# A state-space convolution with gated linear attention on one core: another table for the order of all steps, the engines of evictions and the PSUM rings

## The chip, the cores and the metric

The kernel runs on one core of a Trainium2 chip. The metric is the device time of one execution in microseconds; the median of 3 runs of the kernel before is 265.66 us (265.65 to 267.71). Of the engines, PE is TensorE, DVE VectorE, ACT ScalarE, POOL GpSimd; SP is SyncE, which here only issues DMAs.

## The reference

One input u (1 x 2048 x 512) goes through two branches, which a gate per token mixes into an output of the same shape in bfloat16.

```python
x = A_u                                  # 1 x 2048 x 512, bfloat16
g = _sigmoid((x * gate_w).sum(-1, keepdims=True))
# branch a: per channel d a kernel K of 2048 taps from 128 complex modes, applied as a causal convolution (FFT of length 4096)
P = jnp.exp(logdA[:, :, None] * l[None, None, :])
K = jnp.einsum("dn,dnl,dn->dl", Cc, P, dB).real
y = irfft2(rfft2(up) * rfft2(Kp))[:L]  + u * Dskip
# branch b: 32 heads of 16, feature map phi(q) = [softmax(pq), softmax(-pq)], pq = q @ w_phi per head, no softmax over tokens
kv = einsum("bhsf,bhsd->bhfd", phi_k, v);  z = phi_k summed over s
o = (phi_q @ kv) / (phi_q @ z + 1e-6);  b = o.reshape(B, S, D) @ wo
```

The output is the two branches a and b, mixed token by token with g and 1 - g.

## The kernel before

**Branch a** is worked in 16 units of 32 channels. Four units make a block Q of 128 channels. A unit runs through these steps:

- Tables. TensorE makes arguments (args, L1023 for the sines cs, L1045 for the exponentials E) from statC or statE and a selector table selE (L458); ScalarE turns them into cs and E; VectorE multiplies E into its second half (L1053), builds the products A (L1101, two of 128x2048) and R (L1119, L1123, one each). For 8 of the 16 units, named by the string FOURS, TensorE sums four terms itself; for the other 8, VectorE first halves A by an addition (L1112).
- Kernel taps. TensorE multiplies A and R into kps (L183), the result is evicted as KD.
- Forward transform in two stages: psA (L190), evicted as XA; psB (L196), evicted as XK.
- VectorE multiplies XK with the spectrum of the input, XUX, to t (L1233, L1236). XUX is loaded from DRAM through SyncE (L1186, L1188) into a ring of three.
- Inverse transform: psz (L1265), evicted as Zr, written to DRAM (Zd, L1278) and read back transposed as ZT (L1287). TensorE turns ZT into psy (L1343). VectorE multiplies the result by the gate into xT (L1365, L1368, L1371); in part it goes through a copy into Ctab. The last unit is small enough to stay on the chip: its psz (L1299) is evicted as Z and used directly (L1356). The stores are those of L1382.

**Branch b** runs over 4 blocks of 512 tokens. First for all keys and values: pk (L709) and its exponential Ek on ScalarE, vp (L757) evicted as vb, and their products kvp (L774). Then for the queries: pq (L843), the exponentials Eq, their sums through DRAM (apd, L899; ax, L906), the product Eq by ax on VectorE (L913), ops (L932), and the output product bps with wo (L946, to which L948 and L949 add the convolution's share). The bps are evicted in pieces: a plain copy to xT, and a gated piece of 128x384 by ScalarE (L981) or VectorE (L983), which the store of L995 sends out. The fourth block of tokens is done late, beside the last units.

**What sets the order.** The class Plan (from L71) collects each step as a node with its engine, what it depends on, which buffer rings it takes and gives back. Three strings then decide what is issued where. ORDER holds two digits of base 64 for each node and is the order in which all nodes are emitted; each engine, and each DMA queue, gets its own steps in that order and works them in order. SIDES has a digit for each node that may go to one of two engines: an eviction to ScalarE (L149) or VectorE (L151), the selector table selE and a few others to VectorE or GpSimd, a store to SyncE's or ScalarE's queue. RINGS has a digit for each node that may take its PSUM tile from one of two rings. Nothing in the kernel's functions changes with these strings, only place and engine. The line of Plan.copy that chooses is:

```python
def copy(self, o, i):
    if self.cur.at == "ACT":
        self.nc.scalar.copy(out=o, in_=i)
    else:
        self.nc.vector.tensor_copy(out=o, in_=i)
```

A DMA queue is worked in order too: an issue that waits for its data holds up the issues behind it.

Of the kernel before, what the change touches and what calls it, by code (L numbers as in the profile page):

```python
# [70 lines left out]
class Plan:  # L71

    DIGITS = "0123456789abcdefghijklmnopqrstuvwxyzABCDEFGHIJKLMNOPQRSTUVWXYZ-_"
    ORDER = ("040B0H0K0d0y0C0D0L0s0I070J0M0P0g000S110j0N08010z0T0m0Q0e2R0a0p0q0r0_0W2T100U0O0V14120Y2U2x0A2S050k130Z2y2V2X2Z0R190v0t0u"
             "0b0c0w2_0l0E0X2W1516172L1a061b2Y022-30311y33340n030f0-"
             "0h1e1f0i1w2J18321c0F0o2B2K2M1n1z1H1g1A1o2D2C1d1p1I091x1E1J351Q1R2F1B0x1C2E0G2H1q36372G2I2P382N2Q391F3b2O3c4C1S3a4J4L4K4M"
             "3d3e4Q4R3f4U1Y3g4N1r4O1h4V3h1L4Y4-"
             "4P3i4Z4_3j4W4S53542z57504T3k4X1Z515b5d58521s1D593l5c3n5i5e55565j3m5a1G3o5q5f5g5s5r5t3p3r3q1T5m5n5u3s5v5h5o5k5w5x5B1P4D4E"
             "3w2v5l5p4F5y5F5C3y1U5H3x5G5I5J5z5A1V5D5E3t3z5U3D5K5V5M5N3A3R3E2w3F5W5L1O5_3G5O5Q5X5Y5Z3B3C1W605R5S1N3K3M1K3S1M5-"
             "5P3L634G642A615T653N673T6869626a666m6n6o3U6p3V3W3X3Y6b6c6q6d6r6s1t3Z3H3-1X3_3O1i1j41401_4221431-"  # L80
             "1k1l204445466e272923222b282d4748243P491m2a4a2c2e4b4g2f4c2g4d252h2o4e4h4i4n1u4j3u3v2j4p2i2l2k2m2q2p6i262s4q4o1v4k2n4u2r2t"
             "6f4v4w6j4r3I2u4x4y4z6g4l8l3J4A8p8m6t6u6k6v8q3Q4f4s6x6h8k8o6l8n8r8s6y6z6w6A6C4m4t4B8C6G8t6I6K8w8x8y8u6B6H6J4H8D8v6L6M6N7d"
             "8z8A8E4I8B7e7f8I7g8F6F9e8Q8G8H9b6O6P8R7h7j7i6Q6R8J9f7M7N8S6S6T6U6Vaeaf7O8W8X8K7k9g8L8T8U8Z8-"
             "938M8N7l6D8_7m8V7n6W6X6Y8O8P8Y7P94an7o7pao7q6_70717r90917Qa47S9295ag7R6Z7s6-"
             "72aha8a9966Ea7akaca5ai73aa75979998ajap7677a69aalatamab74ad7TaBaC7t797u7v7U78au7y7z7V7w7x9caq9naras7AavaH7W9d9h9o9paw7X9v"
             "aY9waK7Y7ZaDaL9q9raZ7a9x9y9zaIc57B7-aM9kc69D9EaQaEbX9L7Cb_aF7D9M7_9Ac07EaRaG9iaxaz80ay9B818285bYaA7Ga-"
             "7IaJ86879j9Fc19s7Jb-"
             "9l9m9Na_7bc7aNaOaPc3cbb2b37HbZc283aS9C7FaT849G9H9I9t89aUaWaV8baX7cccc8c99O9u9P9Q9R888cb87Kb9b0c4caceb19J8abacfcgbg8dck9K"
             "8ecl8f8gbbbh8hbcbibob4cP9Sbpbqcd9T8ichci7L8jcBcCcjcsdYcYctcucycDczdZd-cQcR9Ucmd_cHcvcw9W9Xcnbj9VbwbkblbxcocIbre0eLcp9Ze1"
             "e2b5b6eMbse3eUeVcxb7bye4cqbtbu9Ybdbe9-"  # L90
             "9_cAcrcSbme5cZdOdScEbfcFcGcTcUe6a0a1bve7dTdRdWeNa2e8cJcKe9bzbAedeecLeRcNcOa3eSeaebeOcMc_ePbBd0ecd1d7cVd8d9cWeCdfcXeWdPdU"
             "d2daefege-e_eQd3dbdQdgeTdVd4dndodXdhdcg1g2dieDeEdjeXbKfAbCbnbDbEbFeYfBeZf0f1bGc-dpbLddg7dqbHd5f2drbMf3f4f5bNfGbIbJbOezdk"
             "eAfDdsfEeBeIf6f7feffdldtbPdebQdBfCfHehdueifFejdmf8fgeJd6ekdvfIfJdyf9fafhfbg4fifKg5g6dwfjdzfkfcdxdCdEfLdAdFfMg3g8dGg9dHfN"
             "fleFelfdfmfpdDdLgagbgcgddIeGemeKfqeHfOfPfQfRgeenepfneofreqeresgfggghgifSfTfUfofsbRgjbSgkdJftetglfVfYfZgmgngobUbVgqfufWdM"
             "dNbWgpf-fvfxfygreufwevewexbTeydKfzfXf_g0gvgwgsgtgugx")
    SIDES = ("011111010010101011001110110010011001010100001011100000000000011000011001111101000100000100000000000000000000000010000000"
             "00100001000000000000000101010000000000000100001101001")
    RINGS = ("001010111111010010100000000000000000000000100000000000000000001101100000000101101011100100100001101010111100111001010100"
             "01111")
    WARM = ("000000000000000000000000000000000000000000000000000000000000000000000000000000000000000000000000000000000000000000000000"  # L100
            "000000000000000000000")
    FOURS = ("0111100101011000")
# [50 lines left out]
    def run(self):  # L153
        code = {d: i for i, d in enumerate(self.DIGITS)}
        order = [64 * code[a] + code[b] for a, b in zip(self.ORDER[0::2], self.ORDER[1::2])] or list(range(len(self.nodes)))
        assert sorted(order) == list(range(len(self.nodes)))
        sides, rings, warm = iter(self.SIDES), iter(self.RINGS), iter(self.WARM)
        for n in self.nodes:
# [1469 lines left out]
```

## Time and profile before

| what | value |
|---|---|
| median of 3 runs | 265.66 us (265.65 to 267.71) |
| span of the profiled execution | 263.7 us |
| that execution's own time | not given apart from the span; the median stands 1.96 us above it |
| DMA | 35.93 MB, 134 GB/s over the span |
| TensorE steps of the chain that ended last | 32% of the span |
| VectorE steps of that chain | 26% |
| ScalarE steps of that chain | 13% |
| DMA steps of that chain | 12% |

The profile page has the busy time of each engine, the span in slices, the DMA queues, the chain of waits that ended last, and the costliest groups of instructions. The prediction also uses tables of the span cut into stretches, and the timeline of one engine. In the chain a row is a stretch of work, in the order of time; a bracket at the end of a timeline row is the idle time before it and what ended it. The engine that the profile calls SPq or ACTq is the DMA queue of SyncE or ScalarE.

### The profile page before, as it was taken

To read this page: it belongs to the slowest core of one execution; us is meant where nothing else is said; L and a number is where in the kernel's file an instruction comes from. 1 tells how busy PE (TensorE), PEld (TensorE's weight loads), DVE (VectorE), ACT (ScalarE), POOL (GpSimd) and SP (SyncE) were. 2 spreads that over 40 slices of the span, in tenths; PEclk is the share of its full clock that TensorE was granted. 3 is DMA by queue.
4 is the path that set the end of the run, shared out by engine and by line. 5 is a ranking of instruction groups with operands and counts; after the bars stand their busy time and mean duration, and the time that the engine had idled before them with its cause. 6 is when DMAs were issued, how large, how long until landed. Compare 5 with 4: busy or idle time off the path is not lost.

```text
span 263.7 us, 10050 instructions
## 1 busy us (share of the span) xinstructions
PE 198.5 (75%) x4491; PEld 133.8 (51%) x4512; DVE 233.9 (89%) x315; ACT 221.3 (84%) x305; POOL 8.3 (3%) x21
## 2 busy tenths in 40 slices
PE   0755999999845688988565867889996678979770
PEld 0654656646634423446354245665674456764550
DVE  6799989888799989999999999999999999986630
ACT  6989999998899989998999899999998996744200
POOL 4700000000000000000000000000000000000000
PEclk9999999999995659997999579999999999998975
DMA  6899000454500885203343366239753599989576
GB/s 196 144 204 233 6 4 2 121 146 138 151 10 2 239 239 165 83 13 87 88 162 82 122 209 210 73 116 199 150 193 120 189 239 242 179 206 141 133 112 102
DMA packets 67547, 35.93 MB, mean 136 GB/s; under 512 B 46000, under 2 KB 62000, under 8 KB 67504
## 3 DMA queue, kind: packets, MB, share of 16 engines
q1 hardware_dynamic: 65648, 34.76, 55.0%
q10 hardware_dynamic: 1856, 0.52, 1.1%
q8 instruction: 35, 0.57, 1.0%
q14 instruction: 8, 0.07, 0.1%
HBM read 22.17 MB, written 13.11 MB: 134 GB/s over the span
## 4 chain that ended last, share of the span: by engine, by line
PE 32%; DVE 26%; ACT 13%; DMA 12%; issue 7%; SPq 7%; DVEq 0%; ACTq 0%
PE pk L709 5%; DMA ax<-apd 5%; PE vp L757 5%; DVE A L1101 3%; SPq L1494 3%; DMA ZT<-Zd 3%; DMA apd<-apm 3%; ACT cs L68 3%; DVE R L1123 2%; DVE R L1119 2%; PE psz L1265 2%; PE psA L591 2%; PE bps L946 2%; PE psB L616 2%; PE kvp L774 2%
## 5 line engine op out<-in xcount | busy, mean ns | idle before, releaser
L1101 DVE TENSOR_TENSOR A<-Ctab,Dtab 128x2048 bf16<-128x2048 bf16 x32 | 37.9, 1220 | 0.0
L68 ACT ACTIVATE cs<-args 128x1024 bf16<-128x1024 f32 x32 | 30.8, 1042 | 1.5 <-PE args L1023 1.5
L1265 PE MATMUL psz<-t,TI 128*128 128x512 bf16 x51 | 16.5, 414 | 6.2 <-DVE t L1233 4.6
L1123 DVE TENSOR_TENSOR R<-E,cs 128x2048 bf16<-128x2048 bf16 x16 | 19.5, 1219 | 0.1
L1119 DVE TENSOR_TENSOR R<-E,cs 128x2048 bf16<-128x2048 bf16 x16 | 19.5, 1219 | 0.0
L68 ACT ACTIVATE Ek<-pk 128x512 bf16<-128x512 f32 x32 | 16.7, 600 | 1.9 <-PE pk L709 1.6
L183 PE MATMUL kps<-R,A 128*32 128x64 bf16 x1536 | 17.2, 203 | 1.5 <-DVE A L1112 0.4
L183 PEld LDWEIGHTS <-A 128*32 128x32 bf16 x1536 | 15.3, 117 | 5.6 <-issue 2.0
L149 ACT CAST Zr<-psz 128x1024 bf16<-128x1024 f32 x15 | 15.5, 1032 | 3.2 <-PE psz L1265 1.5
L149 ACT CAST XA<-psA 128x1024 bf16<-128x1024 f32 (+1 forms) x15 | 14.7, 1017 | 3.4 <-PE psA L190 3.4
L757 PE MATMUL vp<-WW,xT 128*128 128x512 bf16 x59 | 16.9, 419 | 0.5 <-issue 0.3
L616 PE MATMUL psB<-XAu,TB 64*128 64x128 bf16 x256 | 11.8, 250 | 6.6 <-ACT xst L149 3.5
L1233 DVE TENSOR_TENSOR t<-XUX,XK 128x2048 bf16<-128x2048 bf16 x14 | 16.7, 1219 | 0.0
L68 ACT ACTIVATE E<-args 128x1024 bf16<-128x1024 f32 x16 | 16.4, 1036 | 0.3 <-PE args L1045 0.2
L68 ACT ACTIVATE Eq<-pq 128x512 bf16<-128x512 f32 (+1 forms) x28 | 16.5, 694 | 0.1
L149 ACT CAST XK<-psB 128x1024 bf16<-128x1024 f32 (+1 forms) x14 | 13.7, 993 | 2.8 <-PE psB L196 1.5
L843 PE MATMUL pq<-xT,Wqp 128*128 128x512 bf16 x64 | 15.4, 379 | 0.8 <-ACT xT L149 0.6
L709 PE MATMUL pk<-WW,xT 128*128 128x512 bf16 x58 | 15.0, 380 | 0.4 <-issue 0.2
L190 PE MATMUL psA<-W,KD 128*64 128x128 bf16 x256 | 10.7, 233 | 5.5 <-ACT KD L149 2.7
L616 PEld LDWEIGHTS <-TB 64*128 64x128 bf16 x256 | 9.7, 111 | 9.9 <-issue 9.8
L196 PE MATMUL psB<-XA,TB 128*128 128x128 bf16 (+2 forms) x192 | 10.6, 206 | 3.6 <-DVE XA L151 1.6
L190 PEld LDWEIGHTS <-KD 128*64 128x64 bf16 x256 | 8.5, 117 | 9.1 <-issue 5.2
(210 smaller groups left out, 502.0 us busy)
## 6 DMA issues: line engine op xcount, KB each, us to landing
XUX<-XUd SPq DMA_DIRECT2D x32, 256.0 KB
XUd<-xst SPq DMA_DIRECT2D x8, 512.0 KB
ax<-apd SPq DMA_DIRECT2D x16, 256.0 KB
Zd<-Zr SPq DMA_DIRECT2D x15, 256.0 KB
ZT<-Zd SPq DMA_DIRECT2D x6, 512.0 KB
UD<-in_A_u_dram SPq DMA_DIRECT2D x16, 128.0 KB
XUd<-xst SPq DMA_DIRECT2D x8, 256.0 KB
wqk<-in_B_wqkv_dram SPq DMA_DIRECT2D x1, 1024.0 KB
```

What stands on the lines that cost most here:

```text
L68: return self.nc.scalar.activation(**kw)
L149: self.nc.scalar.copy(out=o, in_=i)
L183: nc.tensor.matmul(kps[32 * dj:32 * dj + 32, g4, e, :], lhsT=A[:, d // 4, 32 * ka:32 * ka + 32, d % 4], rhs=R[:, kr, d, :], start=(i == 0) ...
L190: nc.tensor.matmul(ps[64 * ri:64 * ri + 64], lhsT=lhsT, rhs=fc.W1[:, ri].rearrange("p r d -> p (r d)"), start=True, stop=True, tile_positi ...
L616: nc.tensor.matmul(box.ps[:, c2, sl, :], lhsT=fc.TB[rows, b0:b0 + 2].rearrange("p a b -> p (a b)"), rhs=X.t[rows, k, r0 + sl].rearrange("p ...
L709: nc.tensor.matmul(box.ps[:], lhsT=xT[:, st, kt, :], rhs=g.WW[:, kt, :], start=(kt == 0), stop=(kt == 3))
L757: nc.tensor.matmul(box.ps[:], lhsT=xT[:, st, kt, :], rhs=g.WW[:, 4 + kt, :], start=(kt == 0), stop=(kt == 3))
L1101: nc.vector.tensor_tensor(out=c.A[:, :, 64 * k:64 * k + 64, :].rearrange("p q (x b) l -> p x b q l", b=8), in0=cf.unsqueeze(2).to_broadcas ...
L1119: nc.vector.tensor_tensor(out=c.R[:, :, :, 32:64], in0=t.E[:, 1].unsqueeze(1).to_broadcast([128, 2, 32, 32]), in1=t.cs[:], op=ALU.mult)
L1123: nc.vector.tensor_tensor(out=c.R[:, :, :, 0:32], in0=t.E[:, 0].unsqueeze(1).to_broadcast([128, 2, 32, 32]), in1=t.cs[:, ::-1, :, ::-1], o ...
L1233: nc.vector.tensor_tensor(out=box.t, in0=Ls[r0 // ns].X[:], in1=box.XK[:].unsqueeze(1).to_broadcast([128, 2, 1024]), op=ALU.mult)
L1265: nc.tensor.matmul(box.ps[:, hb, :], lhsT=fc.TI[:, k].rearrange("p t h a -> p (t h a)"), rhs=box.t[:, k, 512 * hb:512 * hb + 512], start=( ...
```

## The change

The three strings ORDER, SIDES and RINGS are replaced; FOURS, WARM and ZPS and every function are the same. The source after is four lines shorter, so that a line number after it is four less than before (L1101 is then L1097). The strings are long, and a line of each shows their kind:

```diff
 class Plan:
...
-    SIDES = ("011111010010101011001110110010011001010100001011100000000000011000011001111101000100000100000000000000000000000010000000"
-             "00100001000000000000000101010000000000000100001101001")
+    SIDES = ("111110110010111010001100101000101000111000001011110000000000111110110001001110000010001000000000000000000000000000000000"
+             "00000000000000000100000000000000000000000001011110101")
-    RINGS = ("001010111111010010100000000000000000000000100000000000000000001101100000000101101011100100100001101010111100111001010100"
-             "01111")
+    RINGS = ("100100101110111011000000000000000000000000100000000000000000111101000000001010101111100111010001001100101011001111100110"
+             "11000")
     FOURS = ("0111100101011000")
```

By these strings, counted over the whole program: VectorE loses two wide evictions XK and one wide XA (128x1024), the selector table selE (to GpSimd, behind Wphi), one bps copy of 256 and the two gated pieces of L983; it gets a copy Ctab of 512, a KD of 256, one XA and one XK of 512, one vb and one copy UDp. ScalarE has the other side of it. Eight of ten vb evictions of VectorE now stand early, of the nine before five. The stores of ScalarE's queue are two instead of four.

The end of VectorE's program, from the last unit's exponential (E, L1053) on, before:

```order
L1053 TENSOR_TENSOR E<-E,Gtab 128x1024
L1123 TENSOR_TENSOR R<-E,cs 128x64x32
L1365 TENSOR_TENSOR xT<-psy,gT 128x4x128
L151 CAST XK<-psB 128x1024
L1368 TENSOR_TENSOR xT<-psy,gT 128x8x128
L1236 TENSOR_TENSOR t<-XUX,XK 128x2x512 x2
L151 CAST XA<-psA 128x32x16
L983 TENSOR_SCALAR xT<-bps,gT 128x384
L151 CAST xT<-bps 128x2x128
L983 TENSOR_SCALAR xT<-bps,gT 128x384
L151 CAST XK<-psB 128x512
L1236 TENSOR_TENSOR t<-XUX,XK 128x2x512 x2
```

and after:

```order
L1049 TENSOR_TENSOR E<-E,Gtab 128x1024
L1097 TENSOR_TENSOR A<-Ctab_75,Dtab 128x64x8x4
L1119 TENSOR_TENSOR R<-E,cs 128x64x32
L1108 TENSOR_TENSOR A<-A 128x8x256
L1361 TENSOR_TENSOR xT<-psy,gT 128x4x128
L147 CAST Ctab_74<-psy 128x4x128
L147 CAST KD<-kps 128x256
L1232 TENSOR_TENSOR t<-XUX,XK 128x2x512 x2
L1364 TENSOR_TENSOR xT<-psy,gT 128x8x128
L147 CAST XA<-psA 128x32x16 x2
L147 CAST XK<-psB 128x512
L1232 TENSOR_TENSOR t<-XUX,XK 128x2x512
```

What moved: both halves of XA and of XK are now VectorE's, the gated pieces are gone from it, the first KD half has come, and the wide XK is gone.

ScalarE around its last change of function table (the row ACT_TABLE_LOAD, after which it makes the last exponentials E), before:

```order
L149 CAST XK<-psB 128x1024
L65 ACT_TABLE_LOAD
L68 ACTIVATE E<-args 128x1024
L149 CAST Zr<-psz 128x2x8x64
L68 ACTIVATE E<-args 128x1024
L149 CAST KD<-kps 128x1024
L149 CAST Zr<-psz 128x2x8x64
L149 CAST XA<-psA 128x32x32 x2
```

and after:

```order
L145 CAST XK<-psB 128x1024 x2
L65 ACT_TABLE_LOAD
L68 ACTIVATE E<-args 128x1024
L145 CAST KD<-kps 128x1024
L145 CAST Zr<-psz 128x2x8x64 x2
L145 CAST oT_4888<-ops 128x1024
L145 CAST XA<-psA 128x32x32 x2
L68 ACTIVATE E<-args 128x1024
```

Between the first and the second E there now stand a KD, two Zr, an oT and two XA, where there was one Zr.

SyncE's queue at the end, before:

```order
L1278 DMA Zd_64_123<-Zr 128x1024
L1382 DMA out_dram<-xT 32x12x256 x2
L995 DMA out_dram<-xT 32x4x384 x2
L1287 DMA ZT<-Zd_64_123 64x32x32 x2
L1382 DMA out_dram<-xT 512x1x64 x4
L995 DMA out_dram<-xT 32x4x384 x2
L1382 DMA out_dram<-xT 512x1x64 x2
```

and after:

```order
L1274 DMA Zd_64_123<-Zr 128x1024
L1378 DMA out_dram<-xT 32x12x256 x2
L991 DMA out_dram<-xT 32x4x384 x2
L1283 DMA ZT<-Zd_64_123 64x32x32 x2
L1378 DMA out_dram<-xT 32x12x128 x2
L1378 DMA out_dram<-xT 512x1x64 x4
L991 DMA out_dram<-xT 32x4x384 x2
L1378 DMA out_dram<-xT 512x1x64 x2
```

Two stores of 32x12x128 have come behind the last ZT loads; two more of 32x12x256, formerly on ScalarE's queue, stand above the piece shown, ahead of the last Zd write.

More of the change, by code (lines that the diff above doesn't have):

```diff
@@ L73 @@
     DIGITS = "0123456789abcdefghijklmnopqrstuvwxyzABCDEFGHIJKLMNOPQRSTUVWXYZ-_"
[L74 to L95, printed above, removed]
@@ L96 @@
-    SIDES = ("011111010010101011001110110010011001010100001011100000000000011000011001111101000100000100000000000000000000000010000000"
-             "00100001000000000000000101010000000000000100001101001")
-    RINGS = ("001010111111010010100000000000000000000000100000000000000000001101100000000101101011100100100001101010111100111001010100"
-             "01111")
+    ORDER = ("190H0I0405060B0C0D0d0e0f0y0z0A0s0t0u000K0L1d0J0M0S0U0V0N0_0P0Q2R11122x0O100W0T13142S0X0Y162T2U0708090g0h0i0j0k0l2y010203"
+             "0m0n0o0a0b0c2V2X0Z15171a1H1b2v0R0-2Y2Z2W2L1c1n1o0p0q0r1w2M2-2_181y302J2K1e1f1p1z1A1I1J2w2B1x1E2D35312E1g1Y2C0v0w0x0E0F0G"
+             "2F321N1B2G2H1C2I33361P372P1O2N341F382Q393b1q1r1s2O4C2z3c4J4K4L4M3d4Y4Z4-3a3e4N4O4_3f4Q3h3g1D4U3j4P1R4R4V4W4S5350573k4T3i"
+             "511S544X52555b5c5d5e3l1G581Q3n595i5f5m3m5g3o1T5n5h5j565a3p3r3s5o1U3q3R5k3S5q5r5s5x1L4D5t3w4E3y5u3x3t3u3v5l5p5B5y5F1V5v5H"
+             "3D1M5C3z2A5w5G3F5z5A5D3G4F5E5I5U5V5W3T3A3B3C3E5X5J5M5N5K5L5O4G5Q5Y5R5Z3K3M5S3U5_1Z635P5T3N5-1h1i1j1k1l1m6067691W643V6162"
+             "65683H3I3J666m3W3L6o3O3P3Q3X3Z3-6a6n6p3Y6b6c1K6q3_6d6r6s414043421X441-27201_4546474828492129224a23246e2d2b252a4b4g4c2e2c"
+             "2f2h1t1u1v266f2j2g4i4d4e4f2i4h4j4k4l4m4n2o2l2q2p6i2k2s4o4p4q4r4s4t2r6j4u4w4v4x2m2t2n6g6k6t4y4z4A6x6u2u8n6y6v4B8r6z8k8o8m"
+             "8q6h6l6w6A6B8l6G8w4H8x8p8t4I6F8s8u6I6K8y6H8z6L8v8A8C9e9f9g8Q6M7d8D8I8E6N6J8R8B7f9b9c9d7g8F6O7h7j6P8S7i8G6Q8H8J8W8Z7Ma_b0"
+             "b17k8K7e6R6S8T6C6D6E7O8-7Q6T8_8L7N7R8M8X6U6V6W937l8O8U8N8V7mae7S8P8Yaf7n7o94907p9192agan7Taoa4ap7q7P6X6Y6Z6_70716-7r7s7t"
+             "a8a995a572ak73ah7u7v7w96aaa6ab9774at98aial7y7z7A7599a776aj9a7x77acau78am797aaqar9n9o7C9v7Uadasav9w7V9paw7B9xaKaLaBaC7D7W"
+             "9q9raHaD9y7X7YaIaQaE9z9D9E7E7F7Zc5c6bXb_9L9Mc0aM7b9k9l9maFaxay9h9i9j9F7-7_80aGazaA7GbYc1aJ7HaR9A9B9C818283858687aNaOaP7I"
+             "7cb-aYaZa-7JaSc784c3aT9Ncb88bZc8899s9t9uc29GaU9H9O8aaVc98b8dc49P9I9J9Kcc8fceaW8gcfaX7Kb5b6b78e8ccacdb8ckb97Lcgch8h8ibg8j"
+             "cBclcibabhcCdYdZbocjcmbpcncDcHbicscvd-cIeLbb9Q9R9S9T9U9Vctcubjcyb2b3b4d_e0bq9W9X9YbccScTcU9Ze1e2eMbwbdbebfcwbke3co9-bxe4"
+             "cPcQcRe5cqczblbmbncxe6e7e8cpbycreUdOeVcVcWcXcAcE9_cFcGa0eNa1dRcJe9eaebdSdTeRdWbrcKbscLcNeOePeSecbzcMcOc_bAdPdQedeeefeWd0"
+             "dUeQbtbubvd1a2d7a3egd8bBbCbDeTdVcYcZc-d2e-d9dad3dfdneXbEbFbGdbe_bKeYbLdgdheZdodXfAf0d4d5d6dcdddefBdpbMdidqf1djehdrfCeibN"
+             "fDf2bHbIbJf4g1f3eCeDeEdkdldmdsdtduf5bOf6fGg2fEf7fHfefFg7fIezeAeBfJffdBg4f8fgfKbPg3f9g5g8g6fLfadvdwdxbQfhdCdydzdAfbfcfddE"
+             "fMdFfiejfNdGg9fjfkfldHekeFeGeHgaeleIeJeKgbepfmfnfoemgcfOfpfqfrfPeneofQbRbSbTeqerdDdIdJdKgdgegfgggifsghgjfRfSfTfUbUbVbWgk"
+             "eseteuevfVfWfXfYfZf-glgmgngodLdMdNftfxfyfzgpfufvfwewexeygqgrf_g0gsgtgugvgwgx")
```

## The prediction

> **What bounds the kernel now.** I read the page's table of engines first, then the span cut into stretches, then the chain that ended last, and at the end the queues that issue the stores. Times without a unit are microseconds. The page's busy line (time, share, instructions):
>
> ```profile
> PE 198.5 (75%) x4491; PEld 133.8 (51%) x4512; DVE 233.9 (89%) x315; ACT 221.3 (84%) x305; POOL 8.3 (3%) x21
> ```
>
> No engine is full over the whole span, so the stretches decide. Their columns are the length, the busy time of PE, PEld, DVE, ACT and POOL with counts, the granted clock, the DMA share and GB/s:
>
> ```profile
> 0.00:30.00 30.00, 15.84 (x170) 13.37 (x172) 25.48 (x58) 26.42 (x34) 8.33 (x21) 1.00 0.88 172
> 30.00:70.00 40.00, 39.47 (x733) 24.24 (x738) 34.88 (x50) 36.95 (x71) 0.00 (x0) 1.00 0.31 88
> 70.00:100.00 30.00, 19.53 (x244) 12.06 (x243) 28.70 (x50) 27.58 (x33) 0.00 (x0) 0.72 0.42 116
> 100.00:215.00 115.00, 88.70 (x2306) 57.80 (x2312) 113.03 (x125) 110.19 (x144) 0.00 (x0) 0.94 0.49 139
> 240.00:250.00 10.00, 7.68 (x185) 4.66 (x185) 5.64 (x10) 3.52 (x6) 0.00 (x0) 1.00 0.80 143
> ```
>
> From 30 to 70 TensorE is busy 39.47 of 40: what VectorE or ScalarE save there is hidden. From 100 to 215 VectorE is busy 113.03 of 115 and ScalarE 110.19: VectorE is the bound, ScalarE a close second with 4.81 to spare. After 240 neither is loaded; the tail is a chain of short steps, as the chain that ended last shows (start, length, what):
>
> ```profile
> 210.97 7.98 DMA ZT<-Zd
> ...
> 236.13 0.94 PE psB L196 x32
> 237.07 0.98 PE kps L183 x48
> ...
> 241.23 0.59 PE psA L190 x16
> 241.84 0.59 ACT XA L149
> 242.46 0.70 DVE XA L151
> 243.20 1.02 PE bps L946 x4
> 244.44 0.86 PE bps L946 x4
> 246.02 0.59 ACT xT L981
> 246.63 0.62 DVE xT L983
> 247.25 0.61 DVE XK L151
> 247.88 1.32 DVE t L1236 x2
> 249.25 3.16 PE psz L1299 x120
> 252.43 0.70 DVE Z L151
> 253.16 0.59 ACT Z L149
> 253.79 0.64 PE psy L1356 x64
> ...
> 256.59 0.69 DVE xT L1368
> ```
>
> The last unit's kernel rows (kps, 16th unit) are done at 238.05 and its inverse transform (psz) starts at 249.25: 11.20 for three small matmul groups and their evictions, with the last attention output (bps) woven in. The last VectorE step ends at 257.28, yet the span is 263.7: the rest is stores (start, length from first issue to the end of the last, queue, line).
>
> ```profile
> 253.16 5.56 ACTq L1382 DMA_DIRECT2D out_dram<-xT  x4
> ```
> ```profile
> 251.63 6.97 SPq L1382 DMA_DIRECT2D out_dram<-xT  x4
> 258.64 1.10 SPq L995 DMA_DIRECT2D out_dram<-xT  x2
> 259.84 1.26 SPq L1382 DMA_DIRECT2D out_dram<-xT  x2
> ```
>
> The store of the last tile is issued at 259.84, 2.56 after that tile is ready, because SyncE works off four older issues and two of L995 first.
>
> **The change part by part.** Lengths come from these groups (busy, mean ns) and from single rows of VectorE's own timeline (start, length), of which the last vb eviction and the wide evictions are shown:
>
> ```profile
> L149 ACT CAST XA<-psA 128x1024 bf16<-128x1024 f32 x14 | 14.1, 1048 | 0.4 <-PE psA L190 0.4
> L149 ACT CAST XK<-psB 128x1024 bf16<-128x1024 f32 x13 | 13.1, 1024 | 1.5 <-PE psB L196 1.5
> L151 DVE CAST vb<-vp 128x512 bf16<-128x512 f32 x9 | 6.1, 687 | 1.9 <-PE vp L757 1.9
> ```
> ```profile
> 57.67 1.22 DVE L458 TENSOR_TENSOR selE<-m,b 128x1024 bf16<-128x1024 bf16 x1
> 98.50 0.68 DVE L151 CAST vb<-vp 128x512 bf16<-128x512 f32 x1
> 171.66 1.22 DVE L151 CAST XK<-psB 128x1024 bf16<-128x1024 f32 x1 [0.40 <-PE psB L196]
> 202.21 1.22 DVE L151 CAST XA<-psA 128x1024 bf16<-128x1024 f32 x1
> 234.34 1.22 DVE L1123 TENSOR_TENSOR R<-E,cs 128x2048 bf16<-128x2048 bf16 x1
> ...
> 237.11 1.23 DVE L151 CAST XK<-psB 128x1024 bf16<-128x1024 f32 x1 [0.25 <-PE psB L196]
> ```
>
> 1, the VectorE stretch. Two evictions leave VectorE for ScalarE inside 100 to 215, the XK at 171.66 and the XA at 202.21: 2 x 1.22 = 2.44 less there (the third wide one, at 237.11, belongs to the tail). Two of the late vb evictions (four before, two now, by the order) go as well, 2 x 0.687 = 1.37, but ahead of 100 (the last is at 98.50), where TensorE's clock is 0.72 and much waits on it; I count them at nothing, and the bound is 2.44 + 1.37 = 3.81. ScalarE takes 1.024 + 1.048 = 2.07 more in the stretch, of its 4.81 to spare. The room is there, but its queue is in order and a moved eviction now stands behind others; I give back a fifth: **-2.0** (ends 0 and -3.8; at 0 ScalarE is the bound).
>
> The selE product at 57.67 goes to GpSimd, and more vb evictions come to VectorE in the early part (eight against five). Both lie in 30 to 70 or before; TensorE's 39.47 of 40 covers them: 0. Without that cover they would cost 3 x 0.69 - 1.22 = +0.8. The new order of the first 30 (sine table work, XUX loads) has the same fate: the DMA share is 0.88 there and TensorE's full stretch begins on what these loads bring: 0, ends -1 and +1.
>
> On GpSimd selE stands behind Wphi:
>
> ```profile
> L473 POOL TENSOR_TENSOR Wphi<-wc,mask 128x512 bf16<-128x512 bf16 x1 | 1.1, 1056 | 4.3 <-DMA wc<-in_B_w_phi_dram 4.3
> L269 DVE TENSOR_SCALAR tgv<-tgc,one 128x1024 int32<-128x1024 f32 x2 | 2.6, 1286 | 2.2 <-ACT TB L68 2.2
> L269 DVE TENSOR_SCALAR tgv<-tgc,if,one 128x1024 int32<-128x1024 f32 x2 | 1.6, 808 | 0.0
> ```
>
> Twice as wide as Wphi, I take 2 x 1.06 = 2.1 of GpSimd for it. A VectorE step of nearly the same form takes 1286 ns where GpSimd runs beside it and 808 where it doesn't, so VectorE may lose about 0.5 per such step, one or two steps, in the hidden part: 0, bound +1. The Trainium skill, "SBUF — State Buffer", section "Who interferes with whom", says that the port pair of VectorE and GpSimd is an exclusive lock, so that one fully blocks the other. By that rule VectorE would stand up to 2.1 rather than 0.5; the rows show a loss of about half of the GpSimd step, less than the rule, and the sum stays as it is, since the place is covered.
>
> 2, the tail chain. Before, two bps groups stand ahead of psA and two between psA and psB, and gated evictions of ScalarE (0.59) and VectorE (0.62) stand ahead of XK. Now all four groups follow kps at once, all four gated evictions are on ScalarE, and VectorE takes both halves of XA (0.70 each) and of XK (the same shape, 0.65 taken), each XK half followed by its own product t. From kps's end at 238.05: four bps groups at 1.1 each (the pair from 243.20 ends at 244.44 + 0.86 = 245.30, so 1.05 a group), 4.4; psA 0.59; XA 2 x 0.70; psB 0.94; XK twice, 1.3, and t twice, 1.32. Sum 4.4 + 0.59 + 1.4 + 0.94 + 2.62 = 9.95 with no waits, against 11.20: 1.25 less, of which I keep a wait of 0.25 back, **-1.0**. Ends: 0, if ScalarE's gated evictions leave the PSUM ring late and TensorE's third group waits for a buffer; -2, if the second halves overlap fully. The VectorE product of psy that moves behind Z (1024 wide, 1.22 like the evictions of that width) falls into the time of the second Z half on ScalarE and the psy group behind it (253.16 to 254.43, 1.27): it costs nothing, and up to 1.2 if that cover is gone. VectorE also gets the first KD half and one Ctab copy of 512; with 5.64 busy of 10 after 240 and the bps groups on TensorE behind kps, they are covered, and 0.4 and 0.7 without that.
>
> 3, the stores. ScalarE's queue has two stores of 32x12x256 and two of 512x1x64; the wide ones go to SyncE, ahead of the last ZT loads, and two of 32x12x128 now stand behind these loads. Behind the last ZT loads SyncE then makes 10 issues instead of 8; the two more cost 1.10 / 2 = 0.55 each (the row at 258.64), 1.1 in all, if SyncE still is behind at the end. On the other side the wide transfers move out of the last 11 and no longer run beside the last stores. I take **0**, ends +1.1 and -1.5 (half of the 2.56 of backlog and some). The Trainium skill, "DMA: Bandwidth & Descriptors", section "Issuing engines are not separate DMA queues", says that transfers of all issuing engines run on the same 16 DMA engines and that a second issuing engine only saves issue time. By that the move can't slow the transfers and costs the 1.1 of issue at most. No row here shows the two cases side by side.
>
> 4, new waits. The table lets the two last exponentials (E of units 14 and 15) come later on ScalarE beside VectorE's order. Adding the groups' mean lengths along each order, an estimate of mine puts the slack between E of unit 14 and its VectorE step at about 8 before and about 0 now. If each of the two E, of the kind and length of a cs step (1.04, the row under the second rival), stands in VectorE's way for a quarter of that, it is **+0.5** (bounds 0 and +2.1); queued behind it on VectorE stand the last A and R products, for which kps and the tail wait. Of SyncE's queue, the first half of the ZT load at 210.97 (7.98 to its landing, in the chain) moves ahead of two Zd writes and the second stays behind them: 0, and up to -1.5 if that landing still sets TensorE's start.
>
> Sum on the profiled execution: 263.7 - 2.0 - 1.0 + 0 + 0.5 = 261.2 of span. The median 265.66 lies 1.96 above this span (the page has no other time for the profiled execution), so **263.2**; as the first two terms have longer ends below (-3.8, -2) than above, I lean by half a microsecond: **262.7** us, 1.1% less.
>
> **The rivals.** First, no change by swallowing: ScalarE becomes the bound. For it: 110.19 of 115 busy, +2.07, and its exponentials now last in line. Against: 4.81 idle. Then term 1 is 0, term 2 is halved by the same ScalarE work ahead of the gated evictions: 265.66 - 0.5 + 0.5 = **265.7**.
>
> Second, slower: the transform loop turns on ScalarE's order. From 100 to 215 each unit's KD, XA and XK evictions sit in ScalarE's queue between table work of this kind:
>
> ```profile
> L68 ACT ACTIVATE cs<-args 128x1024 bf16<-128x1024 f32 x32 | 30.8, 1042 | 1.5 <-PE args L1023 1.5
> ```
>
> If the three moved 1024-wide evictions each wait behind one such step and run there, VectorE's next t product waits 1.04 + 1.02 = 2.06 each, 6.2 in all, against 2.44 saved; with the tail gain gone because E of the last unit is late too (+1.0), the time is 265.66 - 2.44 + 6.2 = 269.4, less what VectorE's other ready work fills: **269**. It decides if VectorE's idle time in 100 to 215 goes over 2 + 2.44 + 2.7 = 7. Against it: before, ScalarE carries 27 such wide evictions of XA and XK (14 and 13 by the groups) behind just such steps, and VectorE still is busy 113.03 of 115.
>
> Third, the change doesn't do what its words say: the table that chooses units whose sums go to TensorE is the same in both, A products and their halving steps have equal counts, and so nothing comes from that. This is sure, and is in the sum as 0. What remains of rival three is that the tail isn't shortened because the end hangs on SyncE's issues alone: term 2 is lost, term 3 is +1.1, the time 265.66 - 2.0 + 0.5 + 1.1 = **265.3**.
>
> **How the numbers follow.** Forecast 262.7 with the terms near their own values: 0.48 (and the better ends, about 259.5, with -3.8 and -2 together: 263.7 - 3.8 - 2 + 1.96 = 259.9, within it). Swallowed by ScalarE or by the stores: 0.32. Slower: 0.20. A measurement of this kernel tells about 1%, 2.66 us, from no change: faster means under 263.0, slower over 268.3. The forecast case holds both sides of 263.0: of its 0.48 I put 0.40 under it, of the 0.32 I put 0.07 there; the slower case is over 268.3 with 0.17. So faster 0.47, same 0.36, slower 0.17. Range 258.8 to 268.5: below by the ends of the first two terms and 1.1 of the stores, above into the slower rival. The forecast's own range is 259.9 to 264.5.
>
> **What would show it.** Right: in 100 to 215 of the new profile VectorE stays over 112 of 115 and does the same work about 2 earlier, so the last R ends near 233.5 rather than 235.56; kps's end to psz's start falls from 11.20 to about 10.2; SyncE's last store stands about as far behind the last tile. Wrong: ScalarE over 113 of 115 with VectorE waiting on XK or E; a psA that starts later than 4.6 after kps; SyncE's last issue more than 3.6 behind the last product; a full TensorE stretch that starts earlier or later than 30 by over 1. The forecast is wrong outright if VectorE's work in its full stretch is not shorter, or if a stall over 3 opens on a load.

## The result, and the profile after

The changed kernel takes 264.24 us (median of 20 runs, 262.80 to 267.72), the kernel before 266.12 us in the 20 runs beside it. The ratio is 0.994, with an interval of 0.9916 to 0.9964: 0.6% faster, about half of the 1.1% that was forecast (262.7 against 265.66), and less than the 1% that the prediction took as the least that can be told from no change. A second measurement of both kernels gave 0.9986 (0.9948 to 1.0023), which does not show the gain by itself. Some executions of either kernel are slower whatever the program, and the ratios leave them out, as the readings below leave out the profiles of outl_act and after_act; in the second measurement this takes away 12 of the 23 runs of the kernel before. Over all runs the medians there are 264.66 and 266.27, a ratio of 0.994.

The page's busy line of the changed kernel:

```profile
PE 195.3 (74%) x4512; PEld 132.4 (50%) x4512; DVE 231.0 (88%) x314; ACT 221.1 (84%) x305; POOL 11.7 (4%) x22
```

VectorE has 2.9 us less work, ScalarE as much as before. The span is 262.7 us. The stretches of the changed kernel, with the columns of the prediction (length, busy time of PE, PEld, DVE, ACT and POOL, granted clock, DMA share, GB/s):

```profile
100.00:215.00 115.00, 89.13 (x2332) 58.85 (x2323) 112.69 (x125) 112.48 (x148) 0.00 (x0) 0.96 0.49 140
230.00:240.00 10.00, 9.85 (x221) 6.61 (x220) 6.11 (x8) 5.30 (x9) 0.00 (x0) 1.00 0.75 189
240.00:250.00 10.00, 7.19 (x248) 5.74 (x248) 5.17 (x8) 2.35 (x4) 0.00 (x0) 0.75 0.87 176
250.00:263.00 13.00, 3.29 (x198) 2.19 (x198) 3.27 (x5) 0.59 (x1) 0.00 (x0) 0.50 0.63 91
```

and two of the kernel before that the prediction does not show:

```profile
230.00:240.00 10.00, 8.35 (x212) 5.81 (x212) 9.07 (x11) 4.40 (x7) 0.00 (x0) 0.83 0.94 186
250.00:263.00 13.00, 5.19 (x294) 4.28 (x286) 2.56 (x5) 0.59 (x1) 0.00 (x0) 0.64 0.72 109
```

Between 100 and 215 VectorE is as busy as before (112.69 against 113.03), and ScalarE took 2.29 more (112.48 against 110.19): the room was there. From 230 on VectorE has little to do (6.11 where it had 9.07), so it finished its full stretch earlier. What follows is seen on its timeline (start, length; the bracket is the idle time before a row and what ended it):

```profile
231.97 1.22 DVE L1108 TENSOR_TENSOR A<-A 128x2048 bf16<-128x2048 bf16 x1
...
238.06 0.69 DVE L1232 TENSOR_TENSOR t<-XUX,XK 128x1024 bf16<-128x1024 bf16 x1 [2.35 <-DMA XUX<-XUd]
239.48 0.69 DVE L1232 TENSOR_TENSOR t<-XUX,XK 128x1024 bf16<-128x1024 bf16 x1 [0.73 <-DMA XUX<-XUd]
240.09 1.22 DVE L1364 TENSOR_TENSOR xT<-psy,gT 128x1024 bf16<-128x1024 f32 x1
241.22 1.28 DVE L147 CAST XA<-psA 128x512 bf16<-128x512 f32 x2
...
254.86 0.69 DVE L1364 TENSOR_TENSOR xT<-psy,gT 128x512 bf16<-128x512 f32 x1 [0.85 <-PE psy L1339]
```

The last operand for kps, now the halving step of A, is ready at 231.97 + 1.22 = 233.19; before it was R at 234.34 + 1.22 = 235.56. That is 2.4 us won. Then VectorE waits twice for a load of XUX, and XA stands behind it. SyncE's queue shows why the load is late, and how the end looks:

```profile
230.20 1.73 SPq L1274 DMA_DIRECT2D Zd<-Zr  x2
231.98 1.87 SPq L1184 DMA_DIRECT2D XUX<-XUd  x4
234.02 5.18 SPq L1283 DMA_DIRECT2D ZT<-Zd  x2
```
```profile
247.84 2.12 SPq L1283 DMA_DIRECT2D ZT<-Zd  x2
250.35 5.23 SPq L1378 DMA_DIRECT2D out_dram<-xT  x6
255.62 1.46 SPq L991 DMA_DIRECT2D out_dram<-xT  x2
258.84 1.25 SPq L1378 DMA_DIRECT2D out_dram<-xT  x2
```

The last four XUX loads are issued together behind two Zd writes, which wait for Zr. In the kernel before, two of them went out ahead of these writes, and the products t that need them came later and did not wait (SyncE's queue, then VectorE):

```profile
222.13 0.88 SPq L1188 DMA_DIRECT2D XUX<-XUd  x2
...
231.35 1.40 SPq L1278 DMA_DIRECT2D Zd<-Zr  x2
232.80 1.89 SPq L1188 DMA_DIRECT2D XUX<-XUd  x2
```
```profile
239.38 1.28 DVE L1236 TENSOR_TENSOR t<-XUX,XK 128x1024 bf16<-128x1024 bf16 x2
```

At the end the last store is issued 258.84 - 255.55 = 3.3 us behind the last product; before it was 2.56. The tail on TensorE:

```profile
234.50 0.72 PE L179 MATMUL kps<-R,A 128*32 128x64 bf16 x64
...
239.92 0.64 PE L186 MATMUL psA<-W,KD 128*64 128x128 bf16 x16
...
242.55 0.95 PE L192 MATMUL psB<-XA,TB 128*128 128x32 bf16 x32 [1.03 <-DVE XA L147]
...
246.34 3.64 PE L1295 MATMUL psz<-TI,t 128*32 128x64 bf16 x128 [1.78 <-DVE t L1232]
```

The way from kps's end (235.22) to psz (246.34) is 11.12, where it was 11.20 and 9.95 to 10.2 had been forecast. When psz starts, the change is 2.9 us ahead of the kernel before; it gives back 1.2 up to the last product and 0.7 behind it. In its second profile it is 1.6 ahead there, as the waits on XUX are longer, and gives back 0.4 and 0.5. Adding up the stages of one profile each, of both kernels and of four runs that are told below, so that each column sums to its span:

| stage, us | before | before, without late stores | change | change, second profile | XUX early | change, without late stores |
|---|---|---|---|---|---|---|
| start to last operand on VectorE | 235.56 | 236.58 | 233.19 | 232.78 | 233.13 | 233.19 |
| last operand to end of kps | 2.49 | 1.53 | 2.03 | 2.29 | 2.18 | 2.33 |
| end of kps to psz | 11.20 | 11.07 | 11.12 | 12.54 | 10.17 | 11.33 |
| psz to end of last product | 8.03 | 8.23 | 9.21 | 8.39 | 10.32 | 8.69 |
| last product to end of span | 6.42 | 4.29 | 7.15 | 6.90 | 6.30 | 5.26 |
| span | 263.7 | 261.7 | 262.7 | 262.9 | 262.1 | 260.8 |

### The profile page after: what moved, and what is told of

It is laid out like the page before. It is cut to its first block, busy times and chain, and to the rows that moved or that the text cites. A ratio compares the mean times of both kernels' runs of the same rounds, so it can differ in the third digit from the quotient of the medians.

```text
span 262.7 us, 10078 instructions
## 1 busy us (share of the span) xinstructions
PE 195.3 (74%) x4512; PEld 132.4 (50%) x4512; DVE 231.0 (88%) x314; ACT 221.1 (84%) x305; POOL 11.7 (4%) x22
## 4 chain that ended last, share of the span: by engine, by line
DVE 35%; ACT 27%; PE 18%; DMA 8%; issue 8%; SPq 1%; DVEq 0%; ACTq 0%
DVE A L1097 7%; DMA XUX<-XUd 4%; DVE t L1229 3%; PE pk L705 3%; ACT Eq L68 3%; ACT XA L145 2%; ACT xst L145 2%; ACT E L68 2%; DMA ax<-apd 2%; DVE XAu L147 2%; DVE R L1119 2%; ACT cs L68 2%; DVE R L1115 2%; ACT Zr L145 2%; DMA pz<-pt 2%
## 5 line engine op out<-in xcount | busy, mean ns | idle before, releaser
L1097 DVE TENSOR_TENSOR A<-Ctab,Dtab 128x2048 bf16<-128x2048 bf16 x32 | 38.7, 1219 | 0.2
L179 PE MATMUL kps<-R,A 128*32 128x64 bf16 x1536 | 18.1, 204 | 8.0 <-DVE A L1097 1.8
L179 PEld LDWEIGHTS <-A 128*32 128x32 bf16 x1536 | 16.3, 118 | 12.0 <-issue 5.6
L1261 PE MATMUL psz<-t,TI 128*128 128x512 bf16 x60 | 15.6, 388 | 2.8 <-DVE t L1229 1.2
L145 ACT CAST XA<-psA 128x1024 bf16<-128x1024 f32 x15 | 15.1, 1042 | 2.6 <-PE psA L186 2.6
L145 ACT CAST XK<-psB 128x1024 bf16<-128x1024 f32 x15 | 15.4, 1035 | 1.6 <-PE psB L192 1.5
L839 PE MATMUL pq<-xT,Wqp 128*128 128x512 bf16 x64 | 16.1, 388 | 0.4 <-ACT Eq L68 0.4
L612 PE MATMUL psB<-XAu,TB 64*128 64x128 bf16 x256 | 9.7, 222 | 8.2 <-ACT xst L145 6.4
L186 PE MATMUL psA<-W,KD 128*64 128x128 bf16 x256 | 10.0, 221 | 5.3 <-ACT cs L68 3.1
L612 PEld LDWEIGHTS <-TB 64*128 64x128 bf16 x256 | 7.8, 97 | 11.0 <-issue 11.0
```

What stands on the lines that cost most here:

```text
L179: nc.tensor.matmul(kps[32 * dj:32 * dj + 32, g4, e, :], lhsT=A[:, d // 4, 32 * ka:32 * ka + 32, d % 4], rhs=R[:, kr, d, :], start=(i == 0) ...
L612: nc.tensor.matmul(box.ps[:, c2, sl, :], lhsT=fc.TB[rows, b0:b0 + 2].rearrange("p a b -> p (a b)"), rhs=X.t[rows, k, r0 + sl].rearrange("p ...
L839: nc.tensor.matmul(box.ps[:, m - m0, :] if late else box.ps[:], lhsT=g.Wqp[:, kt, 128 * m:128 * m + 128], rhs=xT[:, 4 * b:4 * b + 4, kt, : ...
L1097: nc.vector.tensor_tensor(out=c.A[:, :, 64 * k:64 * k + 64, :].rearrange("p q (x b) l -> p x b q l", b=8), in0=cf.unsqueeze(2).to_broadcas ...
L1261: nc.tensor.matmul(box.ps[:, hb, :], lhsT=fc.TI[:, k].rearrange("p t h a -> p (t h a)"), rhs=box.t[:, k, 512 * hb:512 * hb + 512], start=( ...
```

## The experiments

The theory after the result: the gain ahead of the last unit is real and comes from VectorE's two evictions in their new places; the tail gives most of it back. The rivals were that the order alone made the gain, and that the tail's loss is the stores', the clock's or TensorE's own. Ratios are to the kernel before; the changed kernel stands at 0.994 (0.9916 to 0.9964).

**The two evictions back on VectorE** (evict_back), all else as changed; VectorE's order:

```diff
 L1115 TENSOR_TENSOR R<-E,cs 128x64x32
+L147 CAST XK<-psB 128x1024
 L1049 TENSOR_TENSOR E<-E,Gtab 128x1024
...
 L909 TENSOR_TENSOR Eq<-Eq,ax 128x2048
+L147 CAST XA<-psA 128x32x32
 L1049 TENSOR_TENSOR E<-E,Gtab 128x1024
```

> The changed kernel with one wide XK and one wide XA eviction (the two inside 100 to 215) back on VectorE, all else as in the change. If the gain ahead of the last unit comes from VectorE's 2.44 us less of work, the last operand on VectorE comes 2.0 to 2.4 us later than in the change (233.19 there) and the time goes from 264.2 to about 266.3, a ratio to the kernel before of 1.000. If it comes from the order (ScalarE, busy 112.48 of 115 there, is the bound), taking 2.07 us off ScalarE costs nothing or gains: 263.5 to 264.5, a ratio of 0.990 to 0.994.

Measured: 268.14 us, ratio 1.0059 (1.0027 to 1.0092). The last operand comes at 236.57, 3.4 later than in the change, more than the 2.44 of work. VectorE also stands more: between 100 and 215 it is idle 3.39 us instead of 2.31, in these waits among others (of those between 100 and 235: in all, times, longest):

```profile
DVE t L1229 <- ACT XK L145: 1.4, 1, 1.4
DVE A L1097 <- PE kps L179: 0.8, 1, 0.8
```

So in this order the two evictions are worth more than the whole gain; without them the new order is slower than the old one.

**The two evictions moved, in the old order** (before_evict); ScalarE's order:

```diff
 L149 CAST Zr<-psz 128x2x8x64
+L149 CAST XK<-psB 128x1024
 L65 ACT_TABLE_LOAD
...
 L149 CAST Ctab_74<-psy 128x4x128
+L149 CAST XA<-psA 128x32x32
 L149 CAST XK<-psB 128x1024 x2
```

> The kernel before with its wide XK and XA inside 100 to 215 on ScalarE and nothing else changed. If VectorE's work alone is the bound there, the last operand comes about 2.4 us earlier and the ratio is 0.989 to 0.993. If the gain needs the new order to make room on ScalarE, the moved evictions wait behind ScalarE's table work, and the ratio is 0.997 to 1.005.

Measured: 268.34 us, ratio 1.0035 (0.9991 to 1.0080); the last operand is at 238.59, 3.0 later than before. What VectorE waited for between 100 and 235 (in all, times, longest):

```profile
DVE t L1233 <- ACT XK L149: 1.7, 3, 0.9
DVE E L1053 <- ACT E L68: 1.6, 1, 1.6
DVE Eq L913 <- DMA ax<-apd: 1.0, 1, 1.0
DVE oT L151 <- PE ops L932: 0.8, 1, 0.8
```

The first two rows, 3.3 us, are the mechanism of the prediction's slower rival: ScalarE works its steps in order, so its later ones, XK and E, reach VectorE late. The last two are not, since before_ns, with the old evictions, has them too. The interval holds 1, so this half of the change is not shown to be slower, but it does not gain. Neither half of the change gains; both together do.

**XUX early** (xux_early): the four loads go ahead of the two Zd writes; SyncE's order:

```diff
 L1283 DMA ZT<-Zd_0_121 64x32x128 x2
+L1184 DMA XUX<-XUd 128x1024 x4
 L1274 DMA Zd_0_122<-Zr 128x1024 x2
-L1184 DMA XUX<-XUd 128x1024 x4
 L1283 DMA ZT<-Zd_0_122 64x32x64 x2
```

> The changed kernel with the last four XUX loads issued ahead of the two Zd writes instead of behind them. If VectorE's wait on XUX (2.35 and 0.73 us before the two t products of the next to last unit) holds up the last XA behind it, both waits go, the last XA starts up to 0.7 us earlier, and the time falls by 0.5 to 0.7, to about 263.6 (ratio 0.991 to 0.992). If the tail's TensorE order or the stores set the end, or the Zd and ZT transfers come later for it, the time is the same or up to 0.5 more (0.994 to 0.996).

Measured: 263.85 us, ratio 0.9913 (0.9876 to 0.9950); the interval overlaps that of the change, so a gain over it is not shown by the times. The stage is:

```profile
235.70 1.28 DVE L1232 TENSOR_TENSOR t<-XUX,XK 128x1024 bf16<-128x1024 bf16 x2
236.91 1.22 DVE L1364 TENSOR_TENSOR xT<-psy,gT 128x1024 bf16<-128x1024 f32 x1
240.35 1.29 DVE L147 CAST XA<-psA 128x512 bf16<-128x512 f32 x2 [2.23 <-PE psA L186]
```

No wait on XUX is left, XA starts as psA ends (240.31), and kps to psz takes 10.17, as the prediction's sum had it. XA now waits for psA, which stands behind all four bps groups (2.23 us); with two of these behind psA as well, in combo and combo_act below, the way is 9.60. But TensorE then stands for the last ZT load, and the last product comes at 255.80, no earlier than in the change:

```profile
254.61 0.40 PE L1339 MATMUL psy<-ZT,TJ 64*32 64x32 bf16 x32 [1.25 <-DMA ZT<-Zd]
```

**The wide product ahead of Z** (xt_ahead): on VectorE the row `L1364 TENSOR_TENSOR xT<-psy,gT 128x16x64` goes from behind `L147 CAST Z<-psz` to ahead of it.

> The changed kernel with VectorE's 1024-wide product of psy back ahead of Z, in VectorE's idle 4.36 us. If the tail was given back by SyncE's stores, which wait for this product, then the four stores behind it are issued 2 us or more earlier, the last store 1 to 2 us earlier, and the time is 262.5 to 263.2 (ratio 0.987 to 0.990). If the tail was given back by TensorE's lower granted clock (0.50 after 250), or if the last store waits for other things, the time stays at 264.0 to 264.4 (0.993 to 0.995).

Measured: 264.14 us, ratio 0.9944 (0.9910 to 0.9978): no gain. The last product was at 254.93 and the last store was issued at 258.11, 0.6 and 0.7 earlier. The stores did not go 2 us earlier: six of them took SyncE from 249.91 to 256.24.

**Two bps groups behind psA** (bps_split): of the four groups on TensorE two go behind the 16 matmuls of psA, as they stood before.

> The changed kernel with two of the four bps groups put behind psA, as the kernel before had them. If the four groups ahead of psA are what the tail lost (psA starts 4.7 us after kps ends, 3.1 before), psA is 2.2 us earlier, the last XA up to 1 us earlier behind VectorE's work on t and xT, and the time falls by 0.5 to 1. If VectorE's wait on XUX ahead of XA is the limit, psA comes earlier and XA doesn't: time the same, ratio 0.993 to 0.996.

Measured: 265.04 us, ratio 0.9932 (0.9897 to 0.9967), the same as the change. psA ends at 238.95 but XA starts at 241.11, behind VectorE's wait on XUX and the xT product after it, as in the change (241.22): while XUX is late, the order of the bps groups is not what costs. From kps to psz it is 10.12 here, only because kps ends 0.9 later in this profile.

**The last ZT loads ahead of four stores** (zt_first); SyncE's order:

```diff
 L1274 DMA Zd_64_123<-Zr 128x1024
+L1283 DMA ZT<-Zd_64_123 64x32x32 x2
 L1378 DMA out_dram<-xT 32x12x256 x2
 L991 DMA out_dram<-xT 32x4x384 x2
-L1283 DMA ZT<-Zd_64_123 64x32x32 x2
 L1378 DMA out_dram<-xT 32x12x128 x2
```

> The changed kernel with the last two ZT loads issued directly behind the last Zd write, ahead of two stores of 32x12x256 and two of L991. If ZT's late issue (247.84, 1.5 after psz starts; before it was 0.7 ahead of it) sets TensorE's last step, ZT is issued about 2 us earlier and the time falls by 0.5 to 1.5, ratio 0.988 to 0.992. If the last step waits for the Z products and the end for the stores' issues, which stay as many, the time stays (0.993 to 0.996).

Measured: 266.78 us, ratio 1.0037 (0.9995 to 1.0080), so worse than the change. SyncE stands for the Zd write to land with the stores behind it, and the end goes over to the stores, though the last product is 0.6 earlier (254.94):

```profile
SPq L1378 <- DMA out_dram<-xT: 3.2, 2, 3.0
SPq L1283 <- DMA Zd<-Zr: 2.8, 1, 2.8
```

**All four tail edits at once** (combo): XUX early, the product ahead of Z, ZT ahead of the stores, bps split.

> The changed kernel with XUX issued early, the wide product ahead of Z, ZT ahead of the stores and two bps groups behind psA, all at once. If the tail is a chain in which each edit only uncovers the next wait, they gain together what they don't gain singly: psz starts 1.5 to 2 us earlier and the time falls by 1.5 to 3, ratio 0.982 to 0.988. If the end is set by SyncE's 10 issues behind the last ZT load or by TensorE's clock, the gain is under 0.5 (0.992 to 0.994).

Measured: 265.45 us, ratio 1.0006 (0.9967 to 1.0046). psz starts at 244.57, 1.8 earlier than in the change, and the last product is at 253.69, 1.9 earlier; the last store is issued at 259.44, 0.6 later. The whole gain of the chain went into SyncE's queue, as in zt_first, whose edit was slower by itself and is part of this run.

**Stores on ScalarE's queue.** Four runs moved stores: in the changed kernel the last two of L991 (outl_act), the two that the change had moved (stores_back), or six (after_act: two of 32x12x256 and the four of L991, ahead of Z); and the same six in the kernel before (before_act), where the two wide ones were on that queue already and go out earlier. For after_act, ScalarE's order:

```diff
 L977 ACTIVATE xT<-bps,gT 128x384
+L1378 DMA out_dram<-xT 32x12x256 x2
+L991 DMA out_dram<-xT 32x4x384 x4
 L145 CAST Z<-psz 128x64x8
```

> The changed kernel with the last two stores of L991 on ScalarE's queue instead of SyncE's. If the end is SyncE's issue backlog (its last store is issued at 258.84, 3.3 us behind the last product, after a wait of 1.7 on the landing of an earlier store), the last store is issued 1.5 to 3 us earlier and the time is 262 to 263 (ratio 0.984 to 0.989). If the stores' own landing on the shared DMA engines sets the end, a second issuing queue saves only issue time beside other work: 264.0 (0.993).

> The changed kernel with the two 32x12x256 stores that it moved to SyncE back on ScalarE's queue, behind Z as before. If SyncE's issues set the end, two fewer of about 0.65 bring the last store 1.1 to 1.4 us earlier: 262.8 to 263.2, ratio 0.988 to 0.991. If the landing of the stores on the shared DMA engines sets it, the same bytes in another queue change nothing: 0.993 to 0.995.

> The changed kernel with six of SyncE's last stores (two of 32x12x256 and the four of L991) on ScalarE's queue, ahead of Z, where ScalarE has nothing to do. If SyncE's issues set the end, SyncE has six fewer, the last ZT load goes out about 1.5 us earlier, the last store goes right behind the last product (255.5), and the time falls by 3 to 3.5 to about 261, ratio 0.980 to 0.984. If the shared DMA engines set it, it stays within 1 us (0.990 to 0.995).

> The kernel before with its stores of 32x12x256 and the four of L995 on ScalarE's queue ahead of Z. If SyncE's issues set the end of the kernel before as well (last store 2.6 us behind the last product), it gains 1.5 to 2.5, ratio 0.990 to 0.994. If they bind only since the change, it gains under 0.5.

Measured: outl_act 0.9945 (0.9905 to 0.9985), stores_back 0.9967 (0.9939 to 0.9995), after_act 0.9923 (0.9893 to 0.9953), before_act 0.9986 (0.9957 to 1.0015): none is told apart from its own kernel, and each interval lies outside what was expected if SyncE's issues set the end (before_act's expectation ends at 0.994). SyncE's issues alone are not what sets it. after_act is not a clean test, as its stores also go out earlier, beside the last Zd write; the next run shows what that costs. The Trainium skill, "DMA: Bandwidth & Descriptors", section "Issuing engines are not separate DMA queues", says that the issuing engine saves only issue time, as all transfers run on the same 16 DMA engines; these four ratios agree with it, within their intervals.

**The six stores and the tail edits** (combo_act): after_act with XUX early, the product ahead of Z and the bps split.

> The same six stores on ScalarE's queue, with XUX early, the wide product ahead of Z and two bps groups behind psA. If SyncE's issues hid what the tail's other edits gain (the last product was at 253.7 with them, 1.9 us earlier than in the change), the gains now add: the last store behind a product at 253 to 253.7, time 258.5 to 260, ratio 0.970 to 0.977. If not, it equals the run with the stores alone.

Measured: 263.67 us, ratio 0.9899 (0.9863 to 0.9936). It is the best of the runs that write the whole output, though its interval overlaps that of the change, and about 4 us above what was expected. psz starts at 245.55, but the last ZT loads are issued at 250.03, after 3.7 us of waiting for the Zd write to land beside the early stores (a row of SyncE's waits), and TensorE waits again (its timeline):

```profile
SPq L1283 <- DMA Zd<-Zr: 3.7, 1, 3.7
```

```profile
256.16 0.41 PE L1339 MATMUL psy<-ZT,TJ 64*32 64x32 bf16 x32 [1.77 <-DMA ZT<-Zd]
```

**Without the late stores** (after_ns, before_ns): in each kernel twelve late stores are left out, the last eight of 64 KB stay.

```diff
-            n.fn()
+            i in (757, 760, 876, 879, 925, 928) or n.fn()
```

> The changed kernel without twelve of its late stores (all 32x12x256, 32x12x128 and L991 stores of 192 and 96 KB each, so those parts of the output are not written); the last eight of 64 KB stay. If the transfers and issues of these stores take back the tail's gain, the last product comes 1 to 2 us earlier than 255.5, the last store right behind it, and the time falls by 4 to 6 to 258.5 to 260. If the tail's own chain sets the end, it falls by 1.5 to 3 only, the last product staying at 255.

> The kernel before without the same twelve stores (those parts of the output are not written). If the stores took back the change's gain, the pair without them differs by more than the whole kernels do: this one is 2.5 to 3.5 us slower than the changed one without stores, 261.5 to 263.5. If the tail's own chain took it back, they differ by 1 to 2 as the whole kernels do (1.6).

Measured: 261.92 us (0.9892, 0.9843 to 0.9940) and 264.28 us (0.9980, 0.9936 to 1.0025). They differ by 2.4, the whole kernels by 1.9; with such intervals the times can't tell these apart. The profiles, one of each, can: without the stores the changed kernel's last product stands at 255.54, where it stood at 255.55 with them, and that of the kernel before at 257.41, where it stood at 257.28. So the lost time up to the last product is the tail's own chain, as the second case of the expectation has it; what lies behind it shrinks by 1.9 in the one (7.15 to 5.26) and 2.1 in the other (6.42 to 4.29).

**The change again** (after_again), for the scatter; nothing is edited.

> The changed kernel itself a second time, for the scatter of the tail between profiles: the step from psz to the last product was 9.2 us, with psz at 3.6 and a granted clock of 0.50 at the end. If this length is the change's, it is 9.0 to 9.4 again; if it is the clock's, psz may take 2.5 to 3.6 and the step 8.0 to 9.4. Ratio 0.992 to 0.996.

Measured: 264.66 us, ratio 0.9986 (0.9948 to 1.0023), with its stages in the table. The waits on XUX are there again, longer:

```profile
238.54 0.69 DVE L1232 TENSOR_TENSOR t<-XUX,XK 128x1024 bf16<-128x1024 bf16 x1 [2.98 <-DMA XUX<-XUd]
240.73 0.69 DVE L1232 TENSOR_TENSOR t<-XUX,XK 128x1024 bf16<-128x1024 bf16 x1 [1.49 <-DMA XUX<-XUd]
242.47 1.28 DVE L147 CAST XA<-psA 128x512 bf16<-128x512 f32 x2
```

## Why the prediction failed, and where it held

**The sum.** On the profiled execution the forecast was a span of 261.2, and 262.7 was measured. Up to the end of kps the change did 1.3 better than forecast (2.8 for 1.5). Three steps behind it took that back and 1.5 more: term 2 by 0.9, the chain behind psz by 1.2, the stores by 0.7. That the number was not further off is in part luck, since errors of both signs met; the half microsecond by which the forecast was leaned down made the miss larger.

**Right: the bound, and term 1.** VectorE's full stretch sets the last operand, and ScalarE had the room. Terms 1 and 4 together forecast 2.0 - 0.5 = 1.5 us; measured were 2.4 (2.8 in the second profile). Ten profiles that keep the changed order up to there have the last operand between 232.2 and 234.4, three of the old order between 235.6 and 236.6. The back-giving of a fifth and of 0.5 was too careful in this order. The wait on E that term 4 named is there (what VectorE of the changed kernel waited for between 100 and 235: in all, times, longest), but the last operand is 2.4 earlier with it.

```profile
DVE R L1115 <- ACT E L68: 1.5, 2, 1.0
```

**Wrong: term 2, the step from kps to psz, forecast at 1.0 less and measured at 0.1 less.** The sum 4.4 + 0.59 + 1.4 + 0.94 + 2.62 took every step as ready when its engine was. It left out what stands ahead of XA on VectorE: the t products of the unit before, which need XUX. The change issues the first two of these loads at 231.98 instead of 222.13, behind both Zd writes, and lets VectorE come to t right behind the first KD half, where a wide XK and a wide xT product stood ahead of it before (t began at 239.38): 2.35 + 0.73 us of waiting. That VectorE finishes its stretch earlier is not the reason by itself: in evict_back the last operand comes as late as in the kernel before without late stores (236.57 and 236.58), and VectorE waits 0.42 + 2.75 on XUX in the one and not at all in the other; the loads go out later there too, at 235.38. With XUX early the step measures 10.17, the forecast's own length. So the cause of this step's length is shown; the kernel does not gain from it, since the ZT load is next. Two of the prediction's own signs of being wrong are there: psA starts 4.70 after kps (4.6 was named), and the stalls on a load are 3.08 together (3 was named), 4.47 in the second profile. SyncE's and VectorE's new orders held this; the prediction weighed SyncE's queue for stores and one ZT load, not for XUX.

**Left out: the chain behind psz.** It was counted as unchanged, with no reason given but the cover of the wide xT product, and grew from 8.03 to 9.21 (8.39 in the second profile). Four profiles of the old order have 8.03 to 8.29, seven of the new order in which TensorE does not wait for ZT have 8.39 to 9.25, so the growth is not one profile's. Its cause stays open. In the first profile psz itself takes 3.64 instead of 3.14, at a granted clock of 0.75 in 240 to 250 and 0.50 in 250 to 263; before, the clock was 1.00 and 0.64. But a shorter psz does not shorten the chain: xt_ahead has a clock of 1.00 in 240 to 250, a psz of 2.52 and still 8.99; before_ns and before_act have a psz of 2.30 and 2.29 and 8.23 and 8.29. What psz saves there goes into a gap on TensorE behind it, told in the last section. So the lower clock alone is not the cause.

**Term 3, the stores, was mis-sized:** 0 forecast, +0.7 measured (6.42 to 7.15; +0.5 in the second profile), inside its bound of 1.1. But the reason was not only SyncE's two more issues: with them put back (stores_back) 7.45 are left behind the last product.

**What the tail is.** Three chains of nearly equal length end together: VectorE's and TensorE's steps, the way Zr, Zd, ZT through DRAM, and the stores. The experiments that shortened one uncovered another: XUX early, bps_split, combo and combo_act the ZT load (TensorE waits 1.25, 1.85, 0.91 and 1.77 on it), zt_first and combo the stores. Of the rivals, the one that lets the end hang on SyncE's issues alone gave 265.3. It has term 2 lost and the stores longer, as measured, but its reason fell: taking issues off SyncE won nothing that can be measured. The slower one did not come; what it describes is seen only where one order is mixed with the other's evictions.

**The covered parts held.** TensorE is busy 39.96 of 40 between 30 and 70, and the first R ends at 107.83 against 107.51. The cost hidden there was larger than stated: beside selE on GpSimd a VectorE step takes 2.52 instead of 0.81.

## What to carry to other kernels

When an engine's full stretch gets shorter, list what each step behind it waits for, loads included, and look where in the queue these loads stand: the next thing late is often a load that was early enough until now. An eviction moved to an engine with room may gain only with an order that makes the place for it; here neither half alone was faster. Near the end of a kernel, price the last matmuls, the round trip through DRAM and the stores as three chains, since shortening one pays only up to the next.

## What was not expected of the hardware

The prediction took half of GpSimd's time as VectorE's loss, from a mean of 1286 ns over two rows of the kernel before that differ, the first beside Wphi's 1.06 us on GpSimd:

```profile
8.30 1.46 DVE L269 TENSOR_SCALAR tgv<-tgc,one 128x1024 int32<-128x1024 f32 x1 [2.18 <-ACT TB L68]
...
12.81 1.12 DVE L269 TENSOR_SCALAR tgv<-tgc,one 128x1024 int32<-128x1024 f32 x1
```

GpSimd's and VectorE's timelines of the changed kernel:

```profile
10.33 1.90 POOL L454 TENSOR_TENSOR selE<-m,b 128x1024 bf16<-128x1024 bf16 x1
```
```profile
7.99 0.81 DVE L265 TENSOR_SCALAR tgv<-tgc,one 128x1024 int32<-128x1024 f32 x1
...
10.25 2.52 DVE L265 TENSOR_SCALAR tgv<-tgc,one 128x1024 int32<-128x1024 f32 x1 [0.85 <-ACT tgv L286]
```

The step that runs beside selE loses 1.71 of selE's 1.90 us. The Trainium skill, "SBUF — State Buffer", section "Who interferes with whom", has the shared port pair as an exclusive lock; this row agrees with it better than the rows of the kernel before did.

TensorE also shows a gap without a releaser at nearly the same place in most profiles, behind the 56th to 58th matmul of the second psy group that uses Z. It is 0.23 before, 0.95 in before_ns, 0.39 in the first profile of the change and none in the second, 1.49 in xt_ahead, 0.78 in xux_early, none in combo. It tends to be long where psz is short: psz and gap together are 3.2 to 3.4 in the four profiles of the old order, 3.6 to 4.1 in the seven of the new one that do not wait for ZT, and 3.1 to 5.0 in the four that do. What TensorE waits for there stays open.
